# Attention and an MLP mixer on one core: place of the shared row tile, banks of the last sums, loads of two weights

## The chip, the cores and the metric

The kernel runs on one core of one Trainium2 chip. The metric is the device time in microseconds (us) of one execution; the kernel before has a median of 381.32 us over 3 runs (381.31 to 381.64). The profile shows one more execution: TensorE (PE, with its weight loads as PEld), VectorE (DVE), ScalarE (ACT), GpSimd (POOL), and the queues from which transfers are issued, SyncE (SPq), ScalarE (ACTq) and GpSimd (POOLq).

## The reference

8 sequences of 448 tokens, 12 heads of 64 values (768 channels). First cosine attention, then a token MLP over the 448 tokens (256 hidden), then a channel MLP (1536 hidden):

```
q_n = q / (|q| + 1e-6);  k_n = k / (|k| + 1e-6)
attn = softmax(q_n @ k_n.T / tau)
x  = (attn @ v), heads side by side                  # (8, 448, 768)
u  = x + (relu(x.T @ w_tok1) @ w_tok2).T
out = u + relu(u @ w_ch1) @ w_ch2                    # float32
```

## The kernel before, in words

**Pairs of heads.** The work is cut into 48 head pairs, six to a sequence, numbered i. For each pair: load q, k and v; square (`square`, POOL or ACT); sum the squares (`sums`, DVE, tile `ssq`, L266); logarithm and exponential on ACT (`norms`, tiles `rn`, `ne`, L281 and L282); two small DVE steps to the reciprocal length (L275, L279); scale q and k to half precision (`scaled`, POOL, tile `kq`, L302); transpose (`tpose` on PE, psum tile `pst`, copied by DVE into `qk`, L328; from pair 14 on by DMA); four blocks of scores (`score`, psum `psS`, L349) and their exponentials on ACT (`pt`, L350); the product with v (`psO`, L406 or L388) and division (DVE, tile `x`); the first token product (`tok1`, psum `psR`, relu to `rt` on DVE, L427); the second token product with `w2t` (`tok2`, psum `psU`, DVE sum `u`, L441); the transpose of `u` to `ut` (`udma` by DMA, `upose` and `upose_act` through PE).

**The order is written by hand.** Every engine executes in the order in which the program issues. Iterations i = 1 to 5 are a first loop, i = 6 is written out, and i = 7 to 47 are a second loop. In the first loop POOL's order in an iteration is: `scaled(i+1)`, at i = 3 a small rest of the first token weights and else one of the quarters of the first channel weights (`weights_ch1`, L203), `cast_v(i)` (v to half precision), at i = 2 `place_w2` (L198), which writes the second token weights from the loaded tile `w2n` into `w2t` in another column order, and the squares of k of pair i+3. DVE's order is: `ssq(i+2)`, `rt(i-2)`, `x(i-1)`, `rn(i+2)`, `qk(i+1)`, `u(i-2)`. PE's is: two score blocks, `psR(i-2)`, `psO(i-1)`, two score blocks, `pst(i+1)`, `psU(i-2)`. The fourth quarter of the channel weights is issued at the end of iteration 6.

**Weights.** `w2n`, the quarters of `wc1t` and `wc2t` come through POOL's queue, which changes float32 to half precision on the way. In the first loop the loads of q, k and v go through SP.

**Units of the channel MLP.** From i = 7 on PE's spare time is filled from a list `queue` of units: 12 units `m_ch1` to a sequence (psum `psG`, L471) and 2 for each tile of 128 rows of `m_ch2` (psum `psF`, 12 matmuls of 384 columns, L487; then a DVE sum with `u` into `ost`, L491, and a store). Sequences go in twos: 2 x 448 rows are 7 tiles; tile 3 is shared, 64 rows from each sequence, so its DVE sum is two instructions. An iteration has a first slot after three score blocks and, where the account `fed` is due, a second slot after `psQ` and `psU`, then perhaps further ones:

```
unit(True)                 # first slot
... psQ, tok2(i - 2) ...
if due():
    unit(2)                # second slot
while due():
    unit()                 # further slots
tok1(i - 1)
```

The argument says from which pool the psum tile comes: `ps2` has three buffers of two banks, tag "s"; `ps` has two buffers of one bank, tag "b", which `psU`, `psR` and `psO` (two tiles) also take in turn. For tile 3 the expression `wide if m < 3 else wide == 1` gives "s" in the first slot and "b" in the second.

**The end.** The last sequences go through products in seven pieces (`p1` to `p7`, then `q1` to `q7` for five pairs of row tiles g, matmuls in `prod2`, L699). In the last pair (g = 4, row tiles 6 and 3) the sum `psYo` collects `q6`, `q7` and `q4`; `q4` is cut in 256 and 128 columns, each with its DVE sum (`orow`) and its store, the first through SP and the second through ACT.

Of the kernel before, what the change touches and what calls it, by code (L numbers as in the profile page):

```python
# [22 lines left out]
def kernel(  # L23
# [12 lines left out]
    nc = tc.nc  # L36
# [120 lines left out]
    nc.gpsimd.memset(tiny[:], 1e-18)  # L157

    w1t = cst.tile([128, 5, T], FP16, name="w1t")
    w2n = outp.tile([128, TT, S], FP16, name="w2n", tag="ost")  # L160
    w2t = cst.tile([128, TT, S + 64], FP16, name="w2t")
    wc1t = cst.tile([128, DT, C], FP16, name="wc1t")
    wc2t = cst.tile([128, CT, D], FP16, name="wc2t")
# [28 lines left out]
                                in_=moe_w_tok1.rearrange("(p c) t -> c p t", c=NCH)[c, p0:p0 + n])  # L192

    def weights_tok2():
        nc.gpsimd.dma_start(out=w2n[:], in_=moe_w_tok2.rearrange("(tt p) s -> p tt s", p=128))

    def place_w2():
        nc.gpsimd.tensor_copy(out=w2t[:, :, 0:S].rearrange("p t (c s) -> p t c s", c=NCH),  # L198
                              in_=w2n[:].rearrange("p t (s c) -> p t c s", c=NCH))

    def weights_ch1(i):
        cols, t = slice(768 * (i // 2), 768 * (i // 2) + 768), 3 * (i % 2)
        nc.gpsimd.dma_start(out=wc1t[:, t:t + 3, cols],  # L203
                            in_=moe_w_ch1[128 * t:128 * t + 384, cols].rearrange("(t p) c -> p t c", p=128))

    def weights_ch2(i):
        cols = slice(DH * i, DH * (i + 1))
# [306 lines left out]
    def ns(cols, n=1):  # L514
        return n * (cols / 2.4 + 2.5)

    def ch1_units(b):
        return [(ns(S, DT), lambda wide, ct=ct: m_ch1(b, ct, wide)) for ct in range(CT)]

    def ch2_units(b):  # L520
        cuts = ((0, DH, None), (DH, D, 0))
        if b == 0:
            order = [(m, c) for c in cuts for m in range(3)]
        else:
            order = [(m, c) for m in range(3) for c in cuts]
            if b == KEPT_B:
                order = [(3, c) for c in cuts]
            elif b % 2:
                order[5:5] = [(3, cuts[0])]
                order.append((3, cuts[1]))  # L530
        return [(ns(hi - lo, CT), lambda wide, m=m, lo=lo, hi=hi, st=st: m_ch2(b, m, lo, hi, st, wide if m < 3 else wide == 1))
                for m, (lo, hi, st) in order]

    HD, HC = DT // 2, CT // 2
# [4 lines left out]
    def tt(eng, out, a, b, op):  # L539
        eng.tensor_tensor(out=out, in0=a, in1=b, op=op)  # L540
# [123 lines left out]
        return fw["t2"][{4: 4, 5: 1, 6: 2, 7: 3}[n]][j // 2][:, j % 2]  # L664

    TILES = ((7, 8), (0, 1), (2, 9), (4, 5), (6, 3))
    ENDS = ((0, 256), (256, DH))
    sg, xo, yo, zo, eo, orow = {}, {}, {}, {}, {}, {}

    def gtile(t, i):  # L670
# [20 lines left out]
                    4: lambda: (gtile(r1, 1), s[2], ALU.subtract)}[k]()  # L691
        tt(nc.vector, s[k], a, b, op)

    def prod2(n, g, out, start, lo=0, hi=DH):
        r1, r2 = TILES[g]
        a = {1: lambda: gtile(r1, 0), 2: lambda: gtile(r1, 1), 3: lambda: sg[g][4], 4: lambda: gtile(r2, 1),
             5: lambda: sg[g][1], 6: lambda: sg[g][2], 7: lambda: sg[g][3]}[n]()
        for j in range(HC):
            nc.tensor.matmul(out[:, lo:hi], a[:, j], fast_w2(n, j)[:, lo:hi], start=(start and j == 0), stop=(j == HC - 1),  # L699
                             skip_group_check=True)  # L700

    def j3(ap):
        return ap.rearrange("p (j e) -> p j e", e=128)
# [26 lines left out]
        nc.scalar.activation(out=etile2("f5", g), in_=zo[g][:, 0:DH], func=AF.Copy)  # L730

    def q6(g):
        yo[g] = ps2.tile([128, 512], FP32, name=f"psYo_{g}", tag="s")
        prod2(6, g, yo[g], True)
        tt(nc.vector, etile2("f16", g), yo[g][:, 0:DH], eo["f1", g], ALU.add)
        tt(nc.gpsimd, j3(eo["f16", g]), j3(eo["f16", g]), urow(TILES[g][0], 1), ALU.add)

    def f5u(g):
        tt(nc.gpsimd, j3(eo["f5", g]), j3(eo["f5", g]), urow(TILES[g][1], 1), ALU.add)
# [6 lines left out]
        tt(nc.vector, j3(orow[g][0][:, 0:DH]), j3(xo[g][:, 0:DH]), urow(TILES[g][0], 0), ALU.add)  # L746

    def q7(g):
        prod2(7, g, yo[g], False)
        tt(nc.vector, etile2("f167", g), yo[g][:, 0:DH], eo["f1", g], ALU.add)  # L750
        tt(nc.gpsimd, orow[g][1][:, DH:D], eo["f167", g], eo["f5", g], ALU.add)

    def store_row(t, o, lo=0, hi=D, eng=nc.sync):
# [12 lines left out]
        prod2(3, g, zo[g], False)  # L766
        tt(nc.vector, orow[g][0][:, DH:D], zo[g][:, 0:DH], eo["f16", g], ALU.add)

    def q4(g, lo=0, hi=DH):
        prod2(4, g, yo[g], False, lo, hi)  # L770
        tt(nc.vector, orow[g][1][:, lo:hi], yo[g][:, lo:hi], eo["f1u", g][:, lo:hi], ALU.add)

    queue = []
    fed = [0.0, 0.0]

    def unit(wide=False):
        if queue:
            t, fn = queue.pop(0)
            fn(wide)
            fed[0] -= t  # L780

# [8 lines left out]
    def refill(b):  # L790
        new = ch1_units(b) + ch2_units(b)
        if b == 0:
            fed[1] = (sum(t for t, _ in new) - KEPT) / (NPAIR + 1)
        if b == KEPT_B:
            queue[:0] = new[:CT]
            queue[-4:-4], new = new[CT:], []
        queue.extend(new)

    with tc.manual_schedule():
# [11 lines left out]
        load_v(2)  # L811
        load_qk(5)
        load_v(3)
        weights_tok1(0, 7)

        square(0, 1, act=True)
# [7 lines left out]
        norms(0, 0, 1, dve=True)  # L824
        scale_part(0, 0, 0, 2, nc.gpsimd)
        scale_part(0, 0, 2, NCH, nc.gpsimd)
        weights_tok2()
        square(1, 1, act=True)
        square(1, 0, act=True)
        square(2, 1, act=True)  # L830
# [35 lines left out]
        for i in range(1, NPAIR):  # L866
            if i == 1:
                scale(2, 0)
                scale(2, 1, nc.vector)
            else:  # L870
                scaled(i + 1)
                if i == 3:
                    weights_tok1(7, 8)
                else:
                    weights_ch1(max(i - 3, 0))
            load_qk(i + 6)
            score(i, 0)
            score(i, 1)
            sums(i + 2)
            norms(i + 2)  # L880
            if i >= 2:
                tok1(i - 2)
            pv_wide(i - 1)
            x_wide(i - 1)
            norms(i + 2, dve=True)
            cast_v(i)
            if i == 2:
                place_w2()
            square(i + 3, 0)
            if i == 1:  # L890
                warm(10)
            score(i, 2)
            score(i, 3)
            tpose(i + 1)
            if i >= 2:
                tok2(i - 2, pe=True)
            square(i + 3, 1, act=True)
            load_v(i + 4)
            if 2 <= i < 4:
                udma(i - 2)  # L900

        i = NPAIR
        load_qk(i + 6)
# [2 lines left out]
        score(i, 1)  # L906
        sums(i + 2)
        norms(i + 2)
        tok1(i - 2)
        pv_wide(i - 1)  # L910
        x_wide(i - 1)
# [7 lines left out]
        upose_act(i - 4, True)  # L919
        norms(i + 2, dve=True)  # L920
        scaled(i + 2)
        weights_ch1(3)
        tok1(i - 1)


# [24 lines left out]
        for i in range(NPAIR + 1, NP_ALL):  # L950
            b, pj = i // NPAIR, i % NPAIR
            for c in range(KC):
                score(i, c)
                if c == 1 and NPAIR + 2 <= i < NP_ALL - 2:
                    norms(i + 2)
            if i == NPAIR + 1:
                upose(i - 4, 2)
                tok2(i - 2, pe=True)
                pv_wide(i - 1)
                upose_act(i - 2)  # L960
                x_wide(i - 1)
# [12 lines left out]
            if i == NP_ALL - 2:  # L974
                cast_v(i + 1)
                fast_weights1(1, nc.gpsimd)
            fed[1] = RATES.get(i, fed[1])
            if i == NP_ALL - HP:
                fed[1] = (sum(t for t, _ in queue) - fed[0]) / HP
            fed[0] += fed[1]  # L980
            unit(True)
            if old(i):
                score(i, KC)
            else:
                score_rest(i)
            if i in ACT_SQ:
                square(i + 3, 1, act=True)
            if i > NPAIR + 1:
                tok2(i - 2)
            if i + 1 < DMA_T0:  # L990
                tpose(i + 1)
            if due():
                unit(2)
            while due():
                unit()
            tok1(i - 1)
            if i + 3 < NP_ALL:
                sums(i + 3)
            if NP_ALL - 8 <= i < NP_ALL - 5:
                fast_weights2(1, (i - NP_ALL + 8,))  # L1000
            if NP_ALL - 5 <= i < NP_ALL - 3:
                fast_weights2(2, (i - NP_ALL + 5,))
            if i == NP_ALL - 3:
                early.close()
                tail = ctx.enter_context(tc.tile_pool(name="tail", bufs=1, side="right", reuse_waits="tile"))
                tail_tiles()
            if i == NP_ALL - 2:
                fast_g(0, 1)
                fast_g(0, 2)
            if i == NP_ALL - 1:  # L1010
                fast_weights1(4, nc.gpsimd)
# [106 lines left out]
        q3(g)  # L1118
        store_row(TILES[g][0], orow[g][0], DH, D)
        store_row(TILES[g][1], orow[g][1], DH, D, nc.scalar)  # L1120
        for (lo, hi), eng in zip(ENDS, (nc.sync, nc.scalar)):
            q4(g, lo, hi)
            store_row(TILES[g][1], orow[g][1], lo, hi, eng)


# [33 lines left out]
```

## Time and profile before

| | |
|---|---|
| runs | 381.32, 381.31, 381.64 us; median 381.32 |
| profiled execution | 381.85 us, of which 380.1 are the span |
| mean granted PE clock | 0.992 |
| busy | PE 367.0, POOL 286.1, DVE 254.0, ACT 239.1 us |
| chain that ended last, by engine | PE 85%, DVE 5%, POOL 4%, issue 2% |

The span is the time from the first to the last instruction in the profile; 1.75 us of the execution lie outside it. A line of an instruction in order of time has its start, its duration, engine, line and operation, tiles, and in brackets the engine's idle time just before it and what ended it. A line of the chain has start, duration, engine, tile and line.

### The profile page before, as it was taken

To read this page: it belongs to the slowest core of one execution; us is meant where nothing else is said; L and a number is where in the kernel's file an instruction comes from. 1 tells how busy PE (TensorE), PEld (TensorE's weight loads), DVE (VectorE), ACT (ScalarE), POOL (GpSimd) and SP (SyncE) were. 2 spreads that over 40 slices of the span, in tenths; PEclk is the share of its full clock that TensorE was granted. 3 is DMA by queue.
4 is the path that set the end of the run, shared out by engine and by line. 5 is a ranking of instruction groups with operands and counts; after the bars stand their busy time and mean duration, and the time that the engine had idled before them with its cause. 6 is when DMAs were issued, how large, how long until landed. Compare 5 with 4: busy or idle time off the path is not lost.

```text
span 380.1 us, 10313 instructions
## 1 busy us (share of the span) xinstructions
PE 367.0 (97%) x4078; PEld 239.3 (63%) x4078; DVE 254.0 (67%) x568; ACT 239.1 (63%) x413; POOL 286.1 (75%) x413
## 2 busy tenths in 40 slices
PE   6889999999999999999999999999999999999994
PEld 5566666676666665666666666666666675556662
DVE  7788865777436665546645668455657778797872
ACT  5999887855665536753777446787887544255110
POOL 8799998979676676568678587757799754897753
PEclk9899999999999999999999999999999999999998
DMA  7999999989997978876899879999797652103344
GB/s 192 260 250 209 255 248 216 230 148 184 197 227 166 208 164 179 206 161 152 189 203 182 198 183 188 231 170 183 153 198 112 156 98 55 22 1 84 94 127 125
DMA packets 118225, 64.65 MB, mean 170 GB/s; under 512 B 74272, under 2 KB 114848, under 8 KB 118176
## 3 DMA queue, kind: packets, MB, share of 16 engines
q1 hardware_dynamic: 111984, 58.29, 70.3%
q0 software_dynamic: 5616, 5.21, 8.5%
q8 instruction: 32, 0.52, 0.6%
q10 hardware_dynamic: 576, 0.49, 0.5%
q14 instruction: 17, 0.14, 0.2%
HBM read 43.45 MB, written 11.01 MB: 143 GB/s over the span
## 4 chain that ended last, share of the span: by engine, by line
PE 85%; DVE 5%; POOL 4%; issue 2%; DMA 1%; ACT 1%; SPq 0%; DVEq 0%; POOLq 0%; ACTq 0%
PE psG L471 21%; PE psF L487 19%; PE psO L388 9%; PE psS L349 8%; PE psU L438 5%; PE psR L424 5%; PE psYo L699 4%; PE psY L594 3%; PE psZo L699 3%; PE psXo L699 3%; POOL kq L302 2%; PE psQ L356 2%; PE psZ L594 1%; DMA qf<-in_q_dram 1%; PE psO L371 1%
## 5 line engine op out<-in xcount | busy, mean ns | idle before, releaser
L350 ACT ACTIVATE pt<-psS 128x896 f16<-128x896 f32 (+1 forms) x156 | 135.9, 910 | 46.3 <-PE psS L349 46.2
L471 PE MATMUL psG<-ut,wc1t 128*128 128x448 f16 x432 | 89.3, 352 | 0.0
L302 POOL TENSOR_TENSOR kq<-kf,rn 128x384 f16<-128x384 f32 (+1 forms) x47 | 41.8, 888 | 58.1 <-DVE rn L279 58.0
L487 PE MATMUL psF<-wc2t,gt 128*128 128x384 f16 x432 | 75.7, 326 | 0.0
L471 PEld LDWEIGHTS <-wc1t 128*128 128x128 f16 x432 | 40.2, 97 | 32.0
L266 DVE TENSOR_REDUCE ssq<-sq 128x15 f32<-128x960 f32 (+2 forms) x51 | 56.1, 1101 | 3.1 <-POOL kq L302 1.1
L474 ACT ACTIVATE gt<-psG 128x448 f16<-128x448 f32 x72 | 38.9, 540 | 29.0 <-PE psG L471 29.0
L487 PEld LDWEIGHTS <-gt 128*128 128x128 f16 x432 | 40.5, 98 | 24.0
L427 DVE TENSOR_SCALAR rt<-psR 128x256 f16<-128x256 f32 x48 | 20.1, 419 | 47.2 <-PE psR L424 47.1
L302 POOL TENSOR_TENSOR kq<-qf,rn 112x512 f16<-112x512 f32 x45 | 46.9, 1043 | 3.0
L491 DVE TENSOR_TENSOR ost<-psF,u 128x384 f32<-128x384 f32 (+1 forms) x42 | 23.4, 557 | 35.8 <-PE psF L487 33.7
L349 PE MATMUL psS<-qk 64*128 64x448 f16 x312 | 41.6, 357 | 3.3 <-DVE qk L328 2.7
L441 DVE TENSOR_TENSOR u<-psU,x 128x512 f16<-128x512 f32 x48 | 33.1, 690 | 13.1 <-PE psU L438 12.0
L250 POOL TENSOR_TENSOR sq<-kf 128x384 f32<-128x384 f32 (+1 forms) x46 | 40.1, 872 | 1.3 <-DMA kf<-in_k_dram 0.9
L388 PE MATMUL psO<-vt,pt 128*128 128x65 f16 (+1 forms) x1024 | 39.2, 194 | 0.0
L392 DVE TENSOR_TENSOR x<-psO,rec 128x256 f16<-128x256 f32 x82 | 34.8, 425 | 2.8
L388 PEld LDWEIGHTS <-pt 128*128 128x128 f16 (+1 forms) x1024 | 34.2, 97 | 3.5 <-issue 0.9
L250 POOL TENSOR_TENSOR sq<-qf 112x512 f32<-112x512 f32 x30 | 31.1, 1038 | 0.0
L424 PEld LDWEIGHTS <-w1t 128*128 128x128 f16 x384 | 24.8, 98 | 8.6 <-issue 2.1
L438 PE MATMUL psU<-rt,w2t 128*128 128x128 f16 x384 | 29.4, 220 | 0.8 <-DVE qk L328 0.8
L438 PEld LDWEIGHTS <-w2t 128*128 128x128 f16 x384 | 24.8, 98 | 8.4 <-POOL w2t L198 1.0
L424 PE MATMUL psR<-x,w1t 128*128 128x128 f16 x384 | 29.3, 220 | 0.3 <-DVE u L441 0.2
(139 smaller groups left out, 525.1 us busy)
## 6 DMA issues: line engine op xcount, KB each, us to landing
qf<-in_q_dram SPq DMA_DIRECT2D x47, 224.0 KB, 3.8
kf<-in_k_dram SPq DMA_DIRECT2D x36, 192.0 KB, 3.5
vf<-in_v_dram SPq DMA_DIRECT2D x36, 192.0 KB, 3.6
vf<-in_v_dram SPq DMA_DIRECT2D x12, 224.0 KB, 8.3
kf<-in_k_dram SPq DMA_DIRECT2D x11, 224.0 KB, 8.3
wc1t<-in_moe_w_ch_dram POOLq DMA_DIRECT2D x4, 576.0 KB, 11.2
wc2t<-in_moe_w_ch_dram POOLq DMA_DIRECT2D x2, 1152.0 KB, 13.7
out_dram<-ost SPq DMA_DIRECT2D x5, 336.0 KB, 3.7
```

Of the source, the lines that this page charges most:

```text
L250: nc.gpsimd.tensor_mul(out=dst, in0=src, in1=src)
L266: nc.vector.tensor_reduce(out=st["ssq"][0:n, sl], in_=st["sq"][0:n, sl], axis=AXX.X, op=ALU.add)
L302: eng.tensor_tensor(out=kq[0:p, a, 0:n].rearrange("p c g e -> p g c e"), in0=st["kq"[a]][:].rearrange("p (g c) e -> p g c e", g=2), in1=_b ...
L349: nc.tensor.matmul(psS[:, hh, 0:S], qk[hb, c * n:c * n + 128], qm[hb], start=True, stop=True)
L350: nc.scalar.activation(out=pts[i % 2][0:n, 2 * S * c:2 * S * (c + 1)].rearrange("p (h s) -> p h s", h=2), in_=psS[0:n, :, 0:S], func=AF.Ex ...
L388: nc.tensor.matmul(psO[:, m, 0:E + 1], pts[i % 2][0:n, at:at + 128], vt[0:n, i % HP, nch * hh + c, 0:E + 1], start=(old(i) and c == 0), st ...
L424: nc.tensor.matmul(psR[:, tt], w1t[:, w1[m], tt * 128:(tt + 1) * 128], st["x"][:, m], start=(m == 0), stop=(m == 3))
L438: nc.tensor.matmul(psU[:, m], w2t[:, tt, lo:lo + 128], st["rt"][:, tt], start=(tt == 0), stop=(tt == TT - 1))
L471: nc.tensor.matmul(psG[:, 0:S], wc1t[:, dt, ct * 128:(ct + 1) * 128], ut[b][:, dt].rearrange("p m s -> p (m s)")[:, lo:lo + S], start=(dt ...
L474: nc.scalar.activation(out=gt[:, ct, (b % 2) * S:(b % 2 + 1) * S], in_=psG[:, 0:S], func=AF.Relu)
L487: nc.tensor.matmul(psF[:, 0:hi - lo], gt[:, ct, at:at + 128], wc2t[:, ct, lo:hi], start=(ct == 0), stop=(ct == CT - 1))
L699: nc.tensor.matmul(out[:, lo:hi], a[:, j], fast_w2(n, j)[:, lo:hi], start=(start and j == 0), stop=(j == HC - 1), skip_group_check=True)
```

## The change

- **Second token weights**: `w2n` becomes two float32 tiles, loaded by two DMAs on SP's queue just before `weights_tok1`, that is behind `load_v(3)`. `place_w2` becomes two POOL copies from float32 and moves from i = 2 to i = 3. `tok2` in the first loop works on pair i-3 from i = 3 on, with `udma(i-3)`, and iteration 6 does `tok2(3)` ahead of `tok1(4)` beside its own `tok2(4)`.
- **First channel weights**: two halves of 768 columns at i = 2 and i = 4, in place of four quarters at i = 2, 4, 5 and at the end of 6.
- **Shared row tile**: its two units stand earlier in a sequence's list, and the second slot passes over such a unit to the next one if that one may go first. All its psum tiles come with `wide` as given.
- **Last sums**: `psYo` gets two banks. For g = 4 each of `q6`, `q7` and `q4` is 2 x 6 matmuls of 192 columns, one half to a bank, instead of 6 of 384 (`q4`: 6 of 256 and 6 of 128).

```
+    def weights_tok2():
+        for tt in range(TT):
+            nc.sync.dma_start(out=w2n[tt][:, 0:S], in_=moe_w_tok2[128 * tt:128 * tt + 128, :])
     def place_w2():
+        for tt in range(TT):
+            nc.gpsimd.tensor_copy(out=w2t[:, tt, 0:S].rearrange("p (c s) -> p c s", c=NCH),
+                                  in_=w2n[tt][:, 0:S].rearrange("p (s c) -> p c s", c=NCH))
     def weights_ch1(i):
+        cols = slice(C // 2 * i, C // 2 * i + C // 2)
+        nc.gpsimd.dma_start(out=wc1t[:, :, cols], in_=moe_w_ch1[:, cols].rearrange("(t p) c -> p t c", p=128))
...
     def ch2_units(b):
-                order[5:5] = [(3, cuts[0])]
-                order.append((3, cuts[1]))
+                order[3:3] = [(3, cuts[0])]
+                order[5:5] = [(3, cuts[1])]
...
-    def unit(wide=False):
+    def unit(wide=False, late=False):
         if queue:
-            t, fn = queue.pop(0)
+            swap = late and queue[0][2] and len(queue) > 1 and not queue[1][2] and not queue[1][3]
+            t, fn = queue.pop(1 if swap else 0)[:2]
...
-                unit(2)
+                unit(True, True)
...
+    def ycut(g):
+        return 2 if g == len(TILES) - 1 else 1
+    def yprod(n, g, h, start):
+        w = DH // ycut(g)
+        prod2(n, g, yo[g][:, h], start, w * h, w * h + w, 0)
+    def ysum(n, g, start, kind, other):
+        k = ycut(g)
+        for h in range(k):
+            yprod(n, g, h, start)
+        out = etile2(kind, g)
+        tt(nc.vector, out.rearrange("p (h w) -> p h w", h=k), yo[g][:, 0:k, 0:DH // k],
+           other.rearrange("p (h w) -> p h w", h=k), ALU.add)
...
-                else:
-                    weights_ch1(max(i - 3, 0))
+                elif i < 5:
+                    weights_ch1((i - 2) // 2)
...
-            if i == 2:
+            if i == 3:
                 place_w2()
...
-            if i >= 2:
-                tok2(i - 2, pe=True)
+            if i >= 3:
+                tok2(i - 3, pe=True)
...
         norms(i + 2)
+        tok2(i - 3, pe=True)
         tok1(i - 2)
...
-        weights_ch1(3)
         tok1(i - 1)
```

More of the change, by code (lines that the diff above doesn't have):

```diff
@@ L159 @@
     w1t = cst.tile([128, 5, T], FP16, name="w1t")
-    w2n = outp.tile([128, TT, S], FP16, name="w2n", tag="ost")
+    w2n = [outp.tile([128, D], FP32, name=f"w2n{tt}", tag="ost") for tt in range(TT)]
     w2t = cst.tile([128, TT, S + 64], FP16, name="w2t")
@@ L194, in weights_tok2 @@
     def weights_tok2():
-        nc.gpsimd.dma_start(out=w2n[:], in_=moe_w_tok2.rearrange("(tt p) s -> p tt s", p=128))
+        for tt in range(TT):
+            nc.sync.dma_start(out=w2n[tt][:, 0:S], in_=moe_w_tok2[128 * tt:128 * tt + 128, :])
     def place_w2():
-        nc.gpsimd.tensor_copy(out=w2t[:, :, 0:S].rearrange("p t (c s) -> p t c s", c=NCH),
-                              in_=w2n[:].rearrange("p t (s c) -> p t c s", c=NCH))
+        for tt in range(TT):
+            nc.gpsimd.tensor_copy(out=w2t[:, tt, 0:S].rearrange("p (c s) -> p c s", c=NCH),
+                                  in_=w2n[tt][:, 0:S].rearrange("p (s c) -> p c s", c=NCH))
     def weights_ch1(i):
-        cols, t = slice(768 * (i // 2), 768 * (i // 2) + 768), 3 * (i % 2)
-        nc.gpsimd.dma_start(out=wc1t[:, t:t + 3, cols],
-                            in_=moe_w_ch1[128 * t:128 * t + 384, cols].rearrange("(t p) c -> p t c", p=128))
+        cols = slice(C // 2 * i, C // 2 * i + C // 2)
+        nc.gpsimd.dma_start(out=wc1t[:, :, cols], in_=moe_w_ch1[:, cols].rearrange("(t p) c -> p t c", p=128))
     def weights_ch2(i):
@@ L517, in ch1_units @@
     def ch1_units(b):
-        return [(ns(S, DT), lambda wide, ct=ct: m_ch1(b, ct, wide)) for ct in range(CT)]
+        return [(ns(S, DT), lambda wide, ct=ct: m_ch1(b, ct, wide), False, b % 2 == 0) for ct in range(CT)]
     def ch2_units(b):
@@ L528, in ch2_units @@
             elif b % 2:
-                order[5:5] = [(3, cuts[0])]
-                order.append((3, cuts[1]))
-        return [(ns(hi - lo, CT), lambda wide, m=m, lo=lo, hi=hi, st=st: m_ch2(b, m, lo, hi, st, wide if m < 3 else wide == 1))
+                order[3:3] = [(3, cuts[0])]
+                order[5:5] = [(3, cuts[1])]
+        return [(ns(hi - lo, CT), lambda wide, m=m, lo=lo, hi=hi, st=st: m_ch2(b, m, lo, hi, st, wide), m == 3, False)
                 for m, (lo, hi, st) in order]
@@ L666 @@
     TILES = ((7, 8), (0, 1), (2, 9), (4, 5), (6, 3))
-    ENDS = ((0, 256), (256, DH))
     sg, xo, yo, zo, eo, orow = {}, {}, {}, {}, {}, {}
@@ L692, in fast_g, with prod2 @@
         tt(nc.vector, s[k], a, b, op)
-    def prod2(n, g, out, start, lo=0, hi=DH):
+    def prod2(n, g, out, start, lo=0, hi=DH, at=None):
         r1, r2 = TILES[g]
@@ L698, in prod2 @@
         for j in range(HC):
-            nc.tensor.matmul(out[:, lo:hi], a[:, j], fast_w2(n, j)[:, lo:hi], start=(start and j == 0), stop=(j == HC - 1),
+            o = lo if at is None else at
+            nc.tensor.matmul(out[:, o:o + hi - lo], a[:, j], fast_w2(n, j)[:, lo:hi], start=(start and j == 0), stop=(j == HC - 1),
                              skip_group_check=True)
@@ L732, in q6 @@
     def q6(g):
-        yo[g] = ps2.tile([128, 512], FP32, name=f"psYo_{g}", tag="s")
-        prod2(6, g, yo[g], True)
-        tt(nc.vector, etile2("f16", g), yo[g][:, 0:DH], eo["f1", g], ALU.add)
+        yo[g] = ps2.tile([128, 2, 512], FP32, name=f"psYo_{g}", tag="s")
+        ysum(6, g, True, "f16", eo["f1", g])
         tt(nc.gpsimd, j3(eo["f16", g]), j3(eo["f16", g]), urow(TILES[g][0], 1), ALU.add)
+    def ycut(g):
[10 more added lines that the diff above has]
+           other.rearrange("p (h w) -> p h w", h=k), ALU.add)
     def f5u(g):
@@ L748, in q7 @@
     def q7(g):
-        prod2(7, g, yo[g], False)
-        tt(nc.vector, etile2("f167", g), yo[g][:, 0:DH], eo["f1", g], ALU.add)
+        ysum(7, g, False, "f167", eo["f1", g])
         tt(nc.gpsimd, orow[g][1][:, DH:D], eo["f167", g], eo["f5", g], ALU.add)
@@ L767, in q3, with q4 @@
         tt(nc.vector, orow[g][0][:, DH:D], zo[g][:, 0:DH], eo["f16", g], ALU.add)
-    def q4(g, lo=0, hi=DH):
-        prod2(4, g, yo[g], False, lo, hi)
-        tt(nc.vector, orow[g][1][:, lo:hi], yo[g][:, lo:hi], eo["f1u", g][:, lo:hi], ALU.add)
+    def q4(g, h=0):
+        yprod(4, g, h, False)
+        w = DH // ycut(g)
+        lo, hi = w * h, w * h + w
+        tt(nc.vector, orow[g][1][:, lo:hi], yo[g][:, h, 0:w], eo["f1u", g][:, lo:hi], ALU.add)
     queue = []
     fed = [0.0, 0.0]
-    def unit(wide=False):
+    def unit(wide=False, late=False):
         if queue:
-            t, fn = queue.pop(0)
+            swap = late and queue[0][2] and len(queue) > 1 and not queue[1][2] and not queue[1][3]
+            t, fn = queue.pop(1 if swap else 0)[:2]
             fn(wide)
@@ L792, in refill @@
         if b == 0:
-            fed[1] = (sum(t for t, _ in new) - KEPT) / (NPAIR + 1)
+            fed[1] = (sum(u[0] for u in new) - KEPT) / (NPAIR + 1)
         if b == KEPT_B:
@@ L813 @@
         load_v(3)
+        weights_tok2()
         weights_tok1(0, 7)
@@ L826 @@
         scale_part(0, 0, 2, NCH, nc.gpsimd)
-        weights_tok2()
         square(1, 1, act=True)
@@ L894 @@
             tpose(i + 1)
-            if i >= 2:
-                tok2(i - 2, pe=True)
+            if i >= 3:
+                tok2(i - 3, pe=True)
             square(i + 3, 1, act=True)
             load_v(i + 4)
-            if 2 <= i < 4:
-                udma(i - 2)
+            if 3 <= i < 5:
+                udma(i - 3)
         i = NPAIR
@@ L978 @@
             if i == NP_ALL - HP:
-                fed[1] = (sum(t for t, _ in queue) - fed[0]) / HP
+                fed[1] = (sum(u[0] for u in queue) - fed[0]) / HP
             fed[0] += fed[1]
@@ L1120 @@
         store_row(TILES[g][1], orow[g][1], DH, D, nc.scalar)
-        for (lo, hi), eng in zip(ENDS, (nc.sync, nc.scalar)):
-            q4(g, lo, hi)
-            store_row(TILES[g][1], orow[g][1], lo, hi, eng)
+        for h, eng in enumerate((nc.sync, nc.scalar)):
+            q4(g, h)
+            store_row(TILES[g][1], orow[g][1], DH // 2 * h, DH // 2 * (h + 1), eng)
 _INS = ['q', 'k', 'v', 'tau', 'moe_w_tok1', 'moe_w_tok2', 'moe_w_ch1', 'moe_w_ch2']
```

## The prediction, written before the changed kernel had run

> **What bounds the kernel now.** I read the page first: its engine row and its chain.
>
> ```profile
> PE 367.0 (97%) x4078; PEld 239.3 (63%) x4078; DVE 254.0 (67%) x568; ACT 239.1 (63%) x413; POOL 286.1 (75%) x413
> ```
>
> PE is the bound, so what counts is PE's 13 us without work, plus PE work that moves between a stage with idle PE and one without. The chain in order of time shows three kinds of place where it leaves PE: the start up to about 47 us, three places in the middle, and the last 6 us. (A short turn to DVE at 315 us is not touched by the change.) Next, the busy time of the engines by stretches of one iteration each (i = 2 to 6; columns: length, then PE, PEld, DVE, ACT, POOL busy):
>
> ```profile
> 18.27:23.56 5.29, 4.20 (x68) 2.81 (x68) 3.45 (x9) 5.19 (x9) 5.29 (x8) 1.00 1.13 260
> 23.56:27.70 4.14, 3.69 (x68) 2.69 (x65) 4.07 (x9) 4.06 (x7) 4.14 (x7) 1.00 1.15 246
> 32.06:36.43 4.37, 3.91 (x71) 2.86 (x69) 3.77 (x8) 4.34 (x9) 4.37 (x6) 1.00 1.17 273
> 36.43:41.00 4.57, 4.38 (x77) 3.27 (x74) 4.20 (x9) 4.38 (x8) 4.57 (x7) 1.00 1.14 239
> ```
>
> In the start POOL is full, but ACT nearly as much: relief for POOL alone meets ACT next. PE has 0.5 to 1.1 us idle up to i = 5 and only 0.19 in i = 6. Then the chain around the second slot, first with an ordinary unit, then with the shared tile (i = 20):
>
> ```profile
> 126.07 1.95 PE psF L487 x12
> ...
> 129.27 0.86 PE psO L388 x24
> ...
> 132.72 1.96 PE psF L487 x12
> 134.68 0.02 issue
> 134.70 0.55 DVE ost L491
> 135.25 0.01 issue
> 135.27 0.56 DVE ost L491
> 135.83 0.03 issue
> 135.86 0.43 DVE rt L427
> 136.29 0.04 issue
> 136.33 0.28 PE psO L371 x7
> 136.61 0.85 PE psO L388 x24
> ```
>
> The shared unit's psum tile is one of the two "b" buffers; two DVE sums and `rt` stand before `psO` gets its pair of them.
>
> **The middle.** From the end of the second-slot `psF` to `psO` at L388 an ordinary unit takes 129.27 - 128.02 = 1.25 us. At i = 20 it is 136.61 - 134.68 = 1.93, at i = 44 298.23 - 296.28 = 1.95, at i = 21 (with one `psG` of 1.14 between) 144.65 - 142.01 = 2.64 against 2.39. So 0.68 + 0.70 + 0.25 = 1.63 us of stalls. In the built order of the changed program the shared units stand in the first slots of i = 20, 21, 32, 33, 44 and 45, in "s" buffers, and ordinary units take the second slots: the three stalls go. The double sum (1.12 for 0.56) in a first slot is covered by the 2.6 us of `psQ`, `psU` and the second unit, except at i = 45, where no second unit follows. There, before, with an ordinary unit, `psF` ended at 301.04, `rt` at 302.73, and L388 began at 303.06. With 0.56 more on DVE ahead of `u` and `rt`, `rt` ends at 303.29, seven `psO` matmuls (0.28) follow, L388 begins at 303.6: a new stall of 0.5. Other units change places without a change of work. Middle: -1.63 + 0.5 = -1.13; bounds -1.63 (the sum is hidden) and -0.8 (the stall at i = 45 is a whole second sum and `rt` longer).
>
> **The start.** The rows that price it:
>
> ```profile
> L203 POOL DMA_DIRECT2D wc1t<-in_moe_w_ch_dram x4 | 3.2, 803 | 0.0
> L208 POOL DMA_DIRECT2D wc2t<-in_moe_w_ch_dram x2 | 2.2, 1082 | 0.0
> 32.19 1.22 DVE L266 TENSOR_REDUCE ssq<-sq 112x16 f32<-112x1024 f32 x1 [0.35 <-POOL sq L250]
> 36.51 1.22 DVE L266 TENSOR_REDUCE ssq<-sq 112x16 f32<-112x1024 f32 x1 [0.48 <-POOL sq L250]
> ```
>
> POOL's issue of `w2n` (0.81 at 8.5 us) saves nothing: POOL then waited 0.76 for k by DMA. From 20.26 us on, POOL up to the squares of pair 7 (before: 32.1) changes so. Two half issues for two quarter issues: bounds 0.80 (a quarter) and 1.08 (`wc2t`, twice the bytes); I take 0.88, as a half has twice a quarter's row pieces and `wc2t` four times: +0.16. The Trainium skill ("DMA: Bandwidth & Descriptors", section on the anatomy of one DMA on the GpSimd path) says that descriptor generation is small and many can be emitted before the cost shows; by it this term is zero, though 0.80 against 1.08 here says otherwise. Two copies of 448 from float32 for one of 896 (0.98, 0.94 to the next start): a cast of 384 from float32 takes 0.50, one of 512 takes 0.61, so 0.55 each, 1.04 to the next start: +0.10. Together +0.26. `ssq(7)` waits for just these squares (0.35 above), and DVE runs without a gap from there to 36.0, so `qk(6)` and the scores of pair 6 come 0.26 later: 35.50 becomes 35.76.
>
> What goes: at i = 2 `psU(0)` waited 0.81 and ACT lost 0.23 before `pt` at 23.61. What is late next: in i = 3 the copies end at 26.9, `psU(0)` (0.55 to the next start) stands before the scores of pair 4, which then start at 27.5 instead of 27.21, and ACT loses 0.3 there. I count the pair at zero. The issue that falls away at i = 5 would let `ssq(8)` start 0.48 earlier, but then it waits for ACT's square of q at 36.4: zero. The fourth quarter (0.80 at 42.97) lies where PE is full and `kq` has a microsecond and more to spare: zero.
>
> Iteration 6 gets one more `psU` (8 matmuls, 0.45) ahead of `psR(4)` and one more `u` (0.69) between `ssq(8)` and `rt(4)`. PE's cover is its wait of 0.16 for `u(4)` at 39.64 and some 0.2 between the scores of pair 6, which waited for ACT. By hand: scores 35.76, `psU(3)` 36.24, `psR(4)` 36.7, `psO(5)` 37.15, scores 38.26, `psU(4)` 38.73, its `u` until 40.1, `psR(5)` at 40.14 against 39.64. So the start costs +0.5, of which 0.24 is the moved product; from here PE is full and the delay stays. Bounds: -0.25 (ACT's gap is won, the rest hidden) and +1.4 (0.26 + 0.45 + 0.69, nothing hidden).
>
> Transfers: the two `w2n` DMAs stand on SP ahead of v of pair 4 and q, k of pair 6 and put them back by about 1.9 us (SP's issues are 0.95 apart there); k of pair 6 was issued at 16.16, landed after 7.1, and is used at 26.7: 1.5 us are left. `udma(1)` now waits for `u(1)` at 32 with the loads of pair 11 queued behind it on SP; 8.2 us to landing bring it to 41, ahead of the first `psG` at 43.6. The first half is issued at 20.26; POOL's queue moved nothing from 17 to 24 us, then a quarter in some 6: it lands by 36. If it took two full landings (2 x 11.8), 43.9, PE would wait 0.3.
>
> **The end.**
>
> ```profile
> 374.62 0.42 DVE L540 TENSOR_TENSOR orow<-psYo,room 128x256 f32<-128x256 f32 x1
> 374.71 2.71 ACTq L762 DMA_DIRECT2D out_dram<-orow  x4
> 375.10 0.49 PE L699 MATMUL psYo<-t4w,gt_new 128*128 128x128 f16 x6 [0.52 <-DVE orow L540]
> 375.63 0.29 DVE L540 TENSOR_TENSOR orow<-psYo,room 128x128 f32<-128x128 f32 x1 [0.58 <-PE psYo L699]
> ```
>
> PE waits 0.52 until DVE has read the bank. In two banks it does not: the sums of 192 columns (0.36 each, between 0.42 and 0.29) run from 374.62 to 375.36, so DVE ends 0.56 earlier than 375.92. But ACT's queue is busy with its first two issues (0.54 and 0.61) until 375.91; its third went at 376.28 and can now go between 375.95 and 376.28. I take -0.2, nearer the queue than DVE; bounds 0 and -0.56. Twelve matmuls of 192 for six of 384 in `q6` and `q7`: eight of 128 with their own weight loads take 0.45 (56 ns each), six of 384 0.97 (162 ns), so 82 ns each and +0.01 a sum. The skill speaks against the cut ("TensorE: Matmul & The Clock Gate", section on the back-to-back issue gap): 81 ns for a matmul of 128 columns in a stream with weight loads, 131 for 512. By it 192 columns are an estimated 89 ns and the end would cost 0.2 more; the 56 ns here contradict it.
>
> **Sum.** -1.13 + 0.5 - 0.2 = -0.83. The profiled execution is 381.85 (span 380.1 and 1.75 around it), 0.53 above the median; 381.85 - 0.83 = 381.02, and off the median 381.32 the same step gives 380.5.
>
> **Rivals.** *Slower: `w2t` comes too late.* In i = 3 the copies can take 0.95 before the scores of pair 4 delay ACT; beyond that each microsecond goes onto PE and through the squares onto `ssq`. At the dearest POOL row (768 elements in 1.64) 448 take 0.96, two 1.92: +0.9, and with `psU` and `u` unhidden in i = 6 the start costs 0.9 + 1.4 = 2.3; -1.33 + 2.3 = +1.0: 382.3. It decides from a start loss of 2.1 on. Against it: ordinary casts take 0.50 to 0.61. *No change:* the start costs 1.1, about as when only the product and sum moved into i = 6 show: 381.1. For it: DVE has 0.37 idle there, `u` needs 0.69. *A larger gain:* PE's waits take up the moved product and ACT's gap is won: start 0, 380.0. *The end does nothing*, as ACT's queue alone sets it: 380.7; inside the forecast.
>
> **The numbers.** Forecast 0.45, larger gain 0.20, no change 0.21, slower 0.14. A measurement tells about 0.2%, 0.76 us, from no change, so the line lies at 380.56, close above the forecast: 0.33 of its 0.45 go to faster and 0.12 to the same. Faster 0.53, same 0.33, slower 0.14. The range leaves out most of the slower case and the far end of the larger gain (all three terms at their good bounds): 379.7 to 381.7.
>
> **What would show it.** Right: no DVE `ost` or `rt` in the chain at i = 20, 21 and 44; a longer L371 group at i = 45; `psR(5)` some 0.5 later than 39.64; no wait of `psYo` at the end, and the last ACT issue at most 0.4 earlier against PE. Wrong: `psO` still waiting for `ost` in second slots, `psU(0)` waiting for `w2t` over 1.5 us in i = 3, a wait for DMA on k of pair 6 or on `wc1t`, or a start that is no later at all.

## The result, and the profile after

The changed kernel takes 393.57 us (median of 6 runs, 389.64 to 396.36) against 381.31 for the kernel before on the same chip: ratio 1.0269, 95% interval 1.0213 to 1.0325. The two slowest of the six (395.52 and 396.36) count to a slower state and are left out of the ratio and of all differences below, as is one run of the last experiment; the other four have a median of 391.38. The change makes the kernel 10.1 us slower, and the prediction (380.5, range 379.7 to 381.7) is wrong. The profiled execution took 394.25 us, of which 392.5 are the span. Line numbers of the changed kernel are one or two higher than before in most places.

The engine row and the chain by engine say in two lines where to look: no engine worked much longer (PE 368.1 against 367.0), and DMA has 5% of the chain, where it had 1% before.

```profile
PE 368.1 (94%) x4090; PEld 240.3 (61%) x4090; DVE 253.3 (65%) x568; ACT 239.5 (61%) x413; POOL 285.4 (73%) x411
PE 83%; DMA 5%; DVE 5%; ACT 5%; issue 1%; POOL 0%; ACTq 0%; DVEq 0%; POOLq 0%
```

The list of waits (engine, line, releaser: total us, times, longest) names two that the kernel before has not at all (the first) or for 0.9 us only (the second):

```profile
PE psG L472 <- DMA ut<-u: 10.2, 2, 7.6
POOL sq L251 <- DMA kf<-in_k_dram: 10.9, 3, 8.7
```

The chain at this place goes back from the `psG` at 53.91 to a single transfer of 17 us, the DMA transpose of `u` of pair 1:

```profile
36.88 16.99 DMA ut<-u
53.87 0.04 issue
53.91 2.02 PE psG L472 x5
```

The `u` of this pair was ready at 31.6 us. SP's queue shows why the transpose was issued so late all the same (start, time that the issue took). In the kernel before, the two transposes were issued at these times:

```profile
24.02 1.31 SPq L447 DMA_TRANSPOSE ut<-u  x1
...
27.77 1.66 SPq L447 DMA_TRANSPOSE ut<-u  x1
```

In the changed kernel:

```profile
28.76 1.32 SPq L448 DMA_TRANSPOSE ut<-u  x1
30.32 2.75 SPq L140 DMA_DIRECT2D qf<-in_q_dram  x1
33.38 2.48 SPq L117 DMA_DIRECT2D kf<-in_k_dram  x1
35.95 0.83 SPq L117 DMA_DIRECT2D vf<-in_v_dram  x1
36.88 7.31 SPq L448 DMA_TRANSPOSE ut<-u  x1
```

Before, the two transposes landed (their data was there) 8.6 and 7.7 us after their issue, at 32.6 and 35.5. Here they were issued at 28.76 and 36.88 and landed after 17.1 and 17.0, and an issue of a load that takes 0.31 us on an unhindered SP took 2.75 and 2.48. The three loads issued from 30 to 36 us landed after 17 to 20 us. The two halves of the channel weights landed 14.3 and 23.3 us after their issue (the page gives their median):

```profile
wc1t<-in_moe_w_ch_dram POOLq DMA_DIRECT2D x2, 1152.0 KB, 18.8
```

Busy time by stretches of 4 us, in the columns of the prediction's table (the last three are the granted PE clock as a share of full speed, the mean busy share of the 16 DMA engines, and GB/s). Two rows of the kernel before:

```profile
36.00:40.00 4.00, 3.81 (x73) 3.18 (x72) 3.49 (x7) 3.97 (x8) 4.00 (x6) 1.00 1.14 239
40.00:44.00 4.00, 4.00 (x68) 3.06 (x66) 3.02 (x9) 3.55 (x5) 4.00 (x6) 1.00 1.13 255
```

The changed kernel:

```profile
36.00:40.00 4.00, 3.84 (x78) 3.29 (x76) 3.91 (x7) 3.76 (x7) 2.69 (x4) 1.00 0.85 77
40.00:44.00 4.00, 3.32 (x64) 2.57 (x61) 3.02 (x9) 3.56 (x5) 3.98 (x5) 1.00 0.89 70
44.00:48.00 4.00, 0.35 (x1) 0.13 (x2) 1.54 (x3) 0.53 (x2) 0.00 (x0) 0.78 1.51 199
48.00:52.00 4.00, 0.00 (x0) 0.00 (x0) 0.00 (x0) 0.00 (x0) 0.00 (x0) 0.50 0.79 148
56.00:60.00 4.00, 4.00 (x24) 2.29 (x22) 0.62 (x1) 1.82 (x3) 4.00 (x5) 0.51 1.12 317
```

At 40 us PE stands where it stood before (`psR(5)` starts at 39.70 for 39.64). The rate of the transfers, though, is 70 to 77 GB/s from 36 to 44 us, where the kernel before moves 239 to 255. From 48 to 52 us all five engines stand. And when PE resumes, its granted clock is 0.5: the `psG` matmuls take 577 ns for 350, up to 59 us.

For this execution, 12.4 us behind the profiled one of before, these add up nearly. The first `psG` runs at 45.99 and the next, which needs the second transpose, at 53.91, where the kernel before began at 43.3: 10.6 us. From there to the start of `psR(6)`, near the end of the slow stretch, it takes 5.40 us against 2.85: 2.6 from the clock. At i = 8 the kernel stands 13.17 us behind (62.01 against 48.84). The middle gives 1.1 back, and the execution ends 12.4 behind; some 0.3 of this is not assigned.

In the middle, the lag behind the kernel before falls by 0.67 at i = 20, by 0.28 at i = 21 and by 0.71 at i = 44, and grows by 0.54 at i = 45: -1.12 in sum. The chain has no DVE at i = 20 any more, and the predicted new stall at i = 45:

```profile
145.90 1.95 PE psF L488 x12
149.10 0.86 PE psO L389 x24
...
310.82 1.97 PE psF L488 x12
312.78 0.02 issue
312.81 0.55 DVE ost L492
313.36 0.03 issue
313.39 0.56 DVE ost L492
313.95 0.03 issue
313.98 0.69 DVE u L442
314.67 0.34 DVE rt L428
315.01 0.04 issue
315.05 0.28 PE psO L372 x7
315.33 0.86 PE psO L389 x24
```

At the end, in order of time, PE waits for DVE as before (0.49 for 0.52), although the two halves lie in two banks:

```profile
386.82 0.35 DVE L541 TENSOR_TENSOR orow<-psYo,room 128x192 f32<-128x192 f32 x1
387.22 0.66 PE L700 MATMUL psYo<-t4w,gt_new 128*128 128x192 f16 x6 [0.49 <-DVE orow L541]
387.91 0.36 DVE L541 TENSOR_TENSOR orow<-psYo,room 128x192 f32<-128x192 f32 x1 [0.74 <-PE psYo L700]
```

### The profile page after: what moved, and what is told of

Read it like the earlier page. It is cut to its first block, busy times and chain, and to the rows that moved or that the text cites. A ratio compares the mean times of both kernels' runs of the same rounds, so it can differ in the third digit from the quotient of the medians.

```text
span 392.5 us, 10337 instructions
## 1 busy us (share of the span) xinstructions
PE 368.1 (94%) x4090; PEld 240.3 (61%) x4090; DVE 253.3 (65%) x568; ACT 239.5 (61%) x413; POOL 285.4 (73%) x411
## 4 chain that ended last, share of the span: by engine, by line
PE 83%; DMA 5%; DVE 5%; ACT 5%; issue 1%; POOL 0%; ACTq 0%; DVEq 0%; POOLq 0%
PE psG L472 22%; PE psF L488 18%; PE psO L389 9%; PE psS L350 8%; PE psU L439 5%; PE psR L425 4%; DMA ut<-u 4%; PE psYo L700 4%; ACT pt L351 3%; PE psY L595 3%; PE psZo L700 2%; PE psXo L700 2%; PE psQ L357 2%; PE psZ L595 1%; PE psO L372 1%; PE pst L327 1%
## 5 line engine op out<-in xcount | busy, mean ns | idle before, releaser
L472 PE MATMUL psG<-ut,wc1t 128*128 128x448 f16 x432 | 91.5, 358 | 10.2 <-DMA ut<-u 10.2
L251 POOL TENSOR_TENSOR sq<-kf 128x384 f32<-128x384 f32 (+1 forms) x46 | 40.2, 874 | 10.9 <-DMA kf<-in_k_dram 10.9
L350 PE MATMUL psS<-qk 64*128 64x448 f16 x312 | 40.8, 354 | 3.7 <-DVE qk L329 2.9
L442 DVE TENSOR_TENSOR u<-psU,x 128x512 f16<-128x512 f32 x48 | 33.1, 690 | 13.5 <-PE psU L439 12.4
## 6 DMA issues: line engine op xcount, KB each, us to landing
wc2t<-in_moe_w_ch_dram POOLq DMA_DIRECT2D x2, 1152.0 KB, 10.6
```

The source lines that it names most:

```text
L251: nc.gpsimd.tensor_mul(out=dst, in0=src, in1=src)
L350: nc.tensor.matmul(psS[:, hh, 0:S], qk[hb, c * n:c * n + 128], qm[hb], start=True, stop=True)
L472: nc.tensor.matmul(psG[:, 0:S], wc1t[:, dt, ct * 128:(ct + 1) * 128], ut[b][:, dt].rearrange("p m s -> p (m s)")[:, lo:lo + S], start=(dt ...
```

## The experiments

The theory after this reading: the halves keep POOL's queue moving without the pause that the quarters left. Before, that queue moved almost nothing between 30 and 34 us; the transpose of pair 0 landed in this pause, and that of pair 1 just behind it. The rivals: the shift of the second token product (with SP's two loads of `w2n`) makes the transposes late by itself (shift theory); the DMA transposes collide with a half, wherever they stand (collision theory); a half is simply too big (size theory).

**The start of before, the rest changed.** Edit: `weights_tok2`, `place_w2`, `weights_ch1` and the first loop as before.

> The changed kernel with the whole start of the kernel before (second token weights through POOL's queue, one copy at i = 2, second token product of pair i-2, channel weights in quarters); middle and end stay changed. All theories (collision, size, shift) put the loss into the start: the middle's gain of 1.1 us stands alone, the end gives nothing, 380.2 us (379.9 to 380.5). Over 381 us and the middle is not what the profile said.

Measured: 380.52 us (379.85 to 384.47, 10 runs), ratio 0.9984 (0.9954 to 1.0013). The whole loss needs the changed start. Middle and end together bring some 0.8 by the medians, with an interval that reaches no change.

**Quarters again, the other changes kept.** The removed lines are the halves; the fourth quarter is at the end of iteration 6 again (not shown).

```
-                elif i < 5:
-                    weights_ch1((i - 2) // 2)
+                else:
+                    weights_ch1(max(i - 3, 0))
...
```

> The changed kernel with the first channel weights in quarters at their old four places, all else as changed. Collision theory (transposes of u on SP's queue in flight together with a long transfer of POOL's queue slow everything down): the transposes, now at 29 and about 34 us, meet the second quarter for a part of its time, a loss of 0 to 4 us against 380. Size theory (two long transfers without a gap starve the loads): no loss, 380. Shift theory (product and transposes one iteration later are what comes too late): full loss, about 392.

Measured: 382.44 us (381.61 to 384.6), ratio 1.004 (1.0019 to 1.0061). The transposes, issued at 27.75 and 32.00, landed after 7.0 and 12.5 us, and PE waited 0.99 for the second. So 8.9 of the 10.1 us need the halves. The 1.9 against the run just above is what shift, SP loads and copies cost with quarters.

**The halves alone.** Edit: the kernel before with `weights_ch1` in two halves at i = 2 and 4, and nothing else.

> The kernel before with the two halves of the first channel weights at i = 2 and i = 4, all else as before. Collision theory: the transposes at 24 and 28 us fall into the first half's transfer, a loss of 4 us or more, ut landing later than the 8 us of before. Size theory: a loss as well, from loads of q and k landing after 12 us and more. Shift theory: no loss, 381.3.

Measured: 388.07 us (386.96 to 391.42, 4 runs), ratio 1.019 (1.0137 to 1.0243): 6.7 us by themselves. The transposes were issued at 22.85 and 27.40, no later than before, and yet landed after 11.0 and 17.9 us; PE waited 3.0 for the second, and POOL 9.5 for k. The rate fell as in the changed kernel:

```profile
36.00:40.00 4.00, 3.81 (x60) 2.70 (x57) 3.47 (x9) 3.81 (x7) 2.23 (x4) 1.00 0.42 52
40.00:44.00 4.00, 2.33 (x52) 2.04 (x50) 3.31 (x5) 2.64 (x5) 3.47 (x4) 1.00 1.07 95
44.00:48.00 4.00, 2.67 (x10) 0.89 (x10) 0.44 (x2) 1.11 (x4) 0.00 (x0) 0.66 1.12 250
```

The shift by itself is not the cause, then; with the halves it makes matters worse, for 6.7 and 1.9 would give 8.6 and the two together give 10.9 (391.38 - 380.52). Single runs of these kernels lie up to 4.5 us apart, so these 2.3 us are not firm.

**The transposes of pairs 0 and 1 through PE.** Edit: `upose(0, 2)` at the end of i = 5 in place of the two `udma`.

> The changed kernel, but u of pairs 0 and 1 is transposed on PE at the end of iteration 5 (16 transposes and one DVE copy) in place of the two transposes by DMA. Collision theory: no transposes by DMA in the start, loads of q, k, v land within 12 us, no wait of psG; 380.5 to 381.5. Size theory: the loads starve as before, POOL waits for k of pair 10 by 5 us or more, 386 or more. Shift theory: 380.5 to 381.5 too.

Measured: 381.93 us (381.44 to 383.96), ratio 1.0021 (1.0003 to 1.0039), with 233 and 261 GB/s in the two stretches from 36 to 44 us. The loads still landed after 12 to 16 us, and POOL still waited 3.5 for k, with little harm. The halves need the two transposes by DMA to do their damage: loads that land after 12 to 16 us cost little by themselves.

**Plain copies in their place.** SP copies `u` to `ut` without transposing it, in the same place of the queue.

> The changed kernel, but SP copies u of pairs 0 and 1 to ut with the same bytes at the same place in its queue without transposing them (so the channel MLP of the first sequence gets wrong inputs for 256 channels). Collision theory (it is the transposes as such): loads land in 16 us or less, psG waits less than 1.5 us, 381 to 383. Queue theory (SP's queue stands behind the wait for u, whatever is moved): ut still lands late, 386 or more.

Measured: 386.38 us (383.94 to 387.83, 4 runs), ratio 1.012 (1.0065 to 1.0176): between the two theories. The copies landed after 15.3 and 12.1 us, and PE waited 1.9. The rate, however, stayed up:

```profile
36.00:40.00 4.00, 3.54 (x65) 2.60 (x63) 3.62 (x8) 3.90 (x8) 2.60 (x4) 1.00 1.14 237
40.00:44.00 4.00, 3.80 (x71) 3.12 (x69) 3.23 (x8) 3.65 (x6) 3.87 (x4) 1.00 1.15 270
```

So the fall to 70 GB/s needs the transposes, and 5.0 of the 10.1 us go with it (391.38 - 386.38). But 5.2 us stay when nothing is transposed: plain copies at these places of SP's queue are late too while a half moves. In the profiled run much of the rest comes with a low clock, 0.67 from 28 to 32 us and 0.61 from 48 to 52. Against the run with the second half later (below), whose PE waits for no transfer, it is 1.5 us behind at `psR(5)` (41.16 for 39.66), where the first low stretch lies; up to `psR(6)` it loses 3.6 more, of which 1.9 are the wait.

**The middle alone**, on the kernel before.

> The kernel before with the middle of the change alone (place of the shared row tile's units, second slot, psum pools). By the profile after: 0.68, 0.25 and 0.70 us of stalls gone, one of 0.54 new: 1.1 us faster than before, 380.2.

Measured: 380.56 us (379.92 to 384.53, 12 runs), ratio 0.9975 (0.9947 to 1.0002): 0.6 under the 381.13 of the kernel before, where the trace of the changed kernel gave 1.1; the interval just reaches no change. By the medians it is about as much as middle and end together in the first run (380.52), so nothing shows for the end, though a few tenths could hide in the noise.

**Two tiles at the end.** Edit to the first of these kernels: `yo[4]` is two psum tiles of one bank in place of one tile of two, and the earlier sums are two instructions.

```
-        yo[g] = ps2.tile([128, 2, 512], FP32, name=f"psYo_{g}", tag="s")
+        yo[g] = [ps2.tile([128, 512], FP32, name=f"psYo_{g}_{h}", tag="s") for h in range(ycut(g))]
...
```

> The kernel s1_start_before with the two halves of the last sum in two psum tiles in place of two banks of one tile (the two earlier sums then take two DVE instructions each). If PE's wait of 0.49 at the end comes from the two halves being one tile, it is gone, DVE ends 0.4 earlier against PE, and the time is 0.1 to 0.4 below s1_start_before; if ACT's queue alone sets the end, no change against it. 380.2.

Measured: 380.25 us (379.84 to 381.53, 12 runs), ratio 0.9967 (0.9946 to 0.9988), the lowest median of all, and the only interval that lies wholly below the kernel before. Against the first run's 380.52 the 0.3 us are not clear of the noise. In order of time the twelve matmuls and the two DVE sums now run without a wait:

```profile
371.76 1.15 PE L699 MATMUL psYo<-t4w,gt_new 128*128 128x192 f16 x12
372.51 0.80 DVE L540 TENSOR_TENSOR orow<-psYo,room 128x192 f32<-128x192 f32 x2
372.67 2.68 ACTq L775 DMA_DIRECT2D out_dram<-orow  x4
```

It is the dependency of the tile, not of the bank, that made PE wait. But the wait was worth little: from ACT's first issue to its fourth it is 2.08 us here and 2.11 before.

**The second half later.** Edit to the changed kernel: the second half at the end of iteration 6 in place of i = 4.

> The changed kernel with the second half of the first channel weights issued at the end of iteration 6 in place of i = 4. Collision theory: the transposes (issued at about 28 and 33 us) meet only the end of the first half, ut lands within 12 us, most of the loss is gone: 381 to 383. Size theory (a half starves the loads by itself): about half of the loss stays, 385 or more. Queue theory: 386 or more.

Measured: 381.89 us (381.17 to 384.43, 10 runs), ratio 1.0014 (0.9991 to 1.0038). The transposes landed after 8.9 and 6.3 us, the loads issued from 29 to 43 us after 5.1 to 8.7, and PE never waits for a transfer there. So neither the size of a half nor the shift makes the great loss; what does is the second half in flight while the transposes stand in SP's queue. What stays against the run with the start of before (380.52) is 1.4 us.

**The shift alone in the start.** Edit: quarters, and `w2n` through POOL's queue with one copy, as before; only the second token product, its `u` and its transpose stay an iteration later.

> The changed kernel with the quarters of before and with the second token weights of before (one transfer through POOL's queue, one POOL copy from half precision, now at i = 3). Of the changed start only the shift of the second token product, its u and its transpose by one iteration is left. The run with quarters alone undone gave 382.44 us, 1.9 more than the run with the whole start of before (380.52). If the two SP transfers of the second token weights (and the dearer copies) carry those 1.9 us, this one gives 380.5 to 380.9. If the shift carries them, it gives 382.0 to 382.6, and PE's first psG waits for the transpose by DMA of pair 1. Half and half would be 381.5.

Measured: 381.44 us (380.12 to 384.11, 10 runs), ratio 1.0019 (0.9993 to 1.0045). This does not tell the theories apart: the median is the half-and-half value, and the runs reach over all three. In its profile (an execution of 380.52) the transposes landed within 7.7 us and PE waited for none. The traces help here. From the start of the scaling in i = 2 on POOL to `psR(5)` on PE it takes 21.4 to 21.5 us in five profiles with the start of before (one of them with halves), 21.9 with the shift alone, and 22.9 with quarters, where SP's loads and the two copies come in as well: by these single executions the shift carries about 0.4 us, and copies and SP loads about 1.0 (the copies take 1.90 for 0.98). PE's wait of 0.99 for a transpose comes on top.

**The transposes on another queue.**

```
-        nc.sync.dma_start_transpose(out=ut[b][:, pj], ...
+        eng = nc.scalar if i < 2 else nc.sync
+        eng.dma_start_transpose(out=ut[b][:, pj], ...
```

> The changed kernel with one edit: the DMA transposes of u of pairs 0 and 1 are issued by ACT, on a queue that carries nothing else at this time, instead of SP, behind six loads each. Theory that the order in SP's queue is what makes them late: they land some 7 to 9 us after their issue, as before, the first psG waits under 2 us, and the time is 382 to 385. Theory that the 16 DMA engines are what is short while a half is in flight, in whichever queue a transpose stands: it lands 14 to 17 us after its issue all the same, PE waits 8 to 10 us, the GB/s fall below 100 for some 8 us, and the time is 390 to 395.

Measured: 386.04 us (384.33 to 389.04, 3 runs), ratio 1.0132 (1.0072 to 1.0192). That is between the two again, but the trace is clear on the transfers: the halves were issued at the same places (19.34 and 29.80), the transposes landed 8.0 and 11.4 us after their issue in place of 17, the rate stayed at 240 and 247 GB/s from 36 to 44 us, and the first `psG`, at 48.0, waits for no transfer. So it is their place among the loads in SP's queue that makes the transposes so late and lets the rate fall; whether the loads ahead of them or the shared queue does it is not told apart. The new loss is on ACT, which waits for `u` in its turn before it can issue, with the exponentials queued behind:

```profile
28.23 1.27 ACTq L449 DMA_TRANSPOSE ut<-u  x1
29.55 1.73 ACT L351 ACTIVATE pt<-psS 112x896 f16<-112x896 f32 x2 [2.41 <-DVE ssq L267]
34.35 1.21 ACTq L449 DMA_TRANSPOSE ut<-u  x1
35.61 1.72 ACT L351 ACTIVATE pt<-psS 112x896 f16<-112x896 f32 x2 [1.76 <-DVE rec L415]
```

In brackets is ACT's idle time ahead of the exponentials, 2.41 and 1.76, in which these issues lie; the expectation had left that out. Part of the loss is clock again: the granted clock is 0.62 from 28 to 32 us and 0.73 from 36 to 40. The second transpose landed at 45.8; a `psG` at 43.3, as before, would have waited up to some 2.5 us for it (an estimate).

## Why the prediction was wrong

**The step that failed is the paragraph on transfers**, in the sentence "8.2 us to landing bring it to 41". It carried over a landing time from a trace in which the transposes move in or beside a pause of POOL's queue, to a place where that queue is full. It moved a transfer to a later time without asking what the other queue holds then. The `u` was ready when the prediction said (31.6 for 32); but the loads ahead on SP held the issue until 36.88, and the landing took 17.0 us for 8.2, so `ut` was there at 53.9 for 41. The first half landed at 33.3, ahead of the 36 allowed; the second, issued at 29.44, was in flight until 52.7, and of its effect the prediction says nothing. Its count for the same bytes in fewer transfers was POOL's time to issue them, +0.16 us. In truth the halves alone cost 6.7 us, and putting the second one later takes the great loss away.

The evidence was in the trace of before: by stretches, POOL's queue held 79% of the engines' time where a quarter moved (36 to 40 us) and SP's 35%, and from 30 to 34 us, between the quarters, 10% and then 7%. A table of the two queues by stretches, laid under the new issue times, would have shown the transpose of pair 1 and six loads inside a stretch of the first kind.

**No rival named it.** The list had "a wait for DMA on k of pair 6 or on `wc1t`" as a sign of being wrong, but no rival with a transfer that comes late, so no chance and no part of the range stood for it. The slower rival, `w2t` too late, had its condition fulfilled and not its price: the copies take 0.98 each, above its 0.96, and yet the start's compute costs some 1.3 us for its 2.3 (next paragraph); `psU(0)` waits 0.51 and 0.68 for the two copies in i = 3.

**The start's compute** was put at +0.5. Against the one trace of before it shows +0.06 (`psR(5)` at 39.70 for 39.64), but that is luck: the two executions enter the stretch at different times. POOL starts the scaling of i = 2 at 16.98 here and at 18.27 in the trace of before; but other runs whose program is that of before up to this point start it at 16.93 to 17.63, so the lead is no gain of the change, and the reading that dropping POOL's issue of `w2n` "saves nothing" is not refuted. Counted from that entry, `psR(5)` comes after 22.7 us here and after 21.4 to 21.5 with the start of before: +1.3, near the bound of +1.4. The term that was mis-sized is the two copies, put at 1.04 and measured at 1.90; a half's issue was nearly right (0.91 for 0.88). By the median even this alone leaves the range: the run with the second half later, in which PE waits for no transfer, takes 381.89.

**The middle** was right in size and place: three stalls gone (-1.66 in the trace, predicted -1.63) and one new (+0.54, predicted +0.5). **The end** shows no gain in place of -0.2. The rival that expected nothing from the end was right, but for half of its reason: the changed kernel keeps the wait because the tile is one, and without the wait ACT's queue gives at most some hundredths, with a median 0.3 lower that the intervals can't tell from the first run's. The 82 ns of a matmul of 192 columns are as predicted (12 in 0.99 us). The 89 were an estimate from the figures for a stream with weight loads in the Trainium skill ("TensorE: Matmul & The Clock Gate", section on the back-to-back issue gap); the formula of the same section for an isolated matmul, columns / 2.4 + 2.5 ns, gives 82.5, and 56 and 162.5 for the 128 and 384 columns of the prediction's rows (56 and 162).

**Still open:** why transposes in SP's queue take the rate down, and on ACT's queue do not. The fall does not need a half: the kernel before has one too while its transposes are in flight, 74 GB/s from 30 to 32 us, with POOL's queue at 9.7% of the engines' time, and the run with quarters has 105 from 32 to 34 us with no packet of POOL's queue. What the second half changes is that the fall lasts 8 us and more. The two lines are of the kernel before from 30 to 32 us:

```profile
DMA packets 308, 0.15 MB, mean 74 GB/s; under 512 B 199, under 2 KB 308, under 8 KB 308
q0 software_dynamic: 37, 0.02, 9.7%
```

(`q0` is POOL's queue; the columns are packets, MB and the share of the 16 engines' time.)

## What to carry to other kernels

Before two transfers are joined or a transfer is moved, draw the queues by stretches of time and look for what used the pause between them: the queue with the deadline may live in it. Price a moved transfer by the landing times of the stretch that it is moved into, not of the one that it comes from. Two banks in one psum tile were one thing to wait for here; where PE should write one while DVE reads the other, make two tiles. And compare stages of two traces from a common entry point: executions of one program entered this stretch up to 1.3 us apart.

## What was unexpected in the hardware

- Two queues do not share time evenly: where a half moved undisturbed (24 to 28 us in the changed kernel) POOL's queue held 79.2% of the engines' time and SP's 33.6%, with 377 packets each. SP's loads, which landed after 7 to 13 us before, took 11 to 16 us beside the halves without transposes (the run with transposes through PE) and 16 to 20 with them.
- The packets of the type-changing transfer become slow themselves beside transposes in SP's queue: from 40 to 44 us, 148 of them took 75.4% of 16 engines for 4 us, 326 ns each. With the transposes on ACT's queue, from 36 to 40 us, 359 took 75.4%: 134 ns each. Both queues moved nearly the same number of packets while the rate was low as well (136 and 137 from 36 to 40 us), as if they took turns, so that one slow queue holds the other back; no run tests this.
- The granted clock follows a standstill: 0.78, 0.50, 0.50 in the three stretches from 44 to 56 us, and still 0.51 from 56 to 60, though PE worked without a gap from 53.91 on; the price was about 2.6 us on top of a wait of 10.6. The Trainium skill ("TensorE: Matmul & The Clock Gate", part on the clock gate) has the clock at half after an idle window of about 3.4 us and back after at least one such window at work: the half agrees with the 0.50 here, and the `psG` matmuls stayed slow for some 5 us, longer than one window.
- The strided copy from float32 to half precision on POOL takes as long for 448 elements (0.98 us) as the strided copy of 896 within half precision that it replaced (0.98), twice a cast of 384 in plain order (0.50).
